# Moving the weight loads to one queue behind the first transposes, and reordering loads and statistics, in a linear-attention plus GeGLU block

## The chip, the cores and the metric

The kernel runs on one core of one Trainium2 chip. The metric is the device time of one execution in microseconds (us). Engines are named as the profile names them: PE is TensorE, DVE is VectorE, ACT is ScalarE, POOL is GpSimd, SP is SyncE, which here only issues DMAs and DMA transposes.

## The reference, cut to what matters

S = 2048 tokens, D = 448 features, FF = 1792, 16 heads of 28 features. All inputs are bf16.

```python
def _A_ref(x, wqkv, wo):
    q, k, v = split_heads(x @ wqkv)
    phi = lambda t: jnp.where(t > 0, t + 1, jnp.exp(t)) + 1e-6
    pq, pk = phi(q), phi(k)
    kv = jnp.einsum("bhsd,bhse->bhde", pk, v)
    z = jnp.einsum("bhsd->bhd", pk)
    num = jnp.einsum("bhqd,bhde->bhqe", pq, kv)
    den = jnp.einsum("bhqd,bhd->bhq", pq, z)[..., None] + 1e-6
    return merge_heads(num / den) @ wo

def _B_ref(x, w_gate, w_up, w_down):
    return (gelu(x @ w_gate) * (x @ w_up)) @ w_down

h = x + _A_ref(_layernorm(x), A_wqkv, A_wo)
h2 = h + _B_ref(_layernorm(h), B_w_gate, B_w_up, B_w_down)
```

B_x is not used. Two facts order the work. The linear attention needs kv and z summed over all 2048 tokens before the first output, and every matmul that contracts over features needs the normalised tile transposed.

## The kernel before, in words

The 2048 tokens are 16 tiles of 128. The work falls into three stages that overlap.

**A1.** For each tile t: batch-norm statistics on DVE (`ln_stats`, L432 to L434), 1/sqrt on ACT (`ln_rstd_act`, L441), then the normalisation into a slot of `xn` (XN_R = 6 slots), on DVE for the first four tiles (L467) and on POOL after them (L470), and a copy of the last 64 columns on DVE (`dup`, L472). The transposition into `xnT` is done by PE and a DVE evacuation for the first four tiles (L480, L483, one PSUM bank, 7) and by a DMA transpose issued from SP for the other twelve (L485). Then follow the K and V projections (`fk`, L496, and `fv`, L504 to L508; tiles 0 and 1 alone, the rest in pairs), the feature map of K (exp on ACT L522, clip on POOL L525, `pk` on DVE L527), the evacuation of V on ACT (L529) and the sum of kv (`fnacc`, L535). K has four PSUM banks, V two. The 16 Q projections (L560, four tiles and a quarter of the features each) have their own exp, clip and `pqT` (L563 to L565).

**A2.** For each tile (`a2_tile`, L568): numerator and denominator (L580), the division (L583, L584), the transposition of the result (PE for tiles 0 and 1, L594; a DMA transpose from SP for the rest, L599), the product with wo (L607), the residual (L610), the second statistics, the second normalisation (L622 or L625), a copy that doubles the row (`wrap`, L627) and the transposition into `hnT` (PE with an ACT evacuation for tiles 0 and 1, L634 and L637; DMA transposes from SP for the rest, L640).

**B.** `gu_chunk` (L665): gate and up products in 64-row halves of PE (L690, L692), gelu on ACT (L714), the product on DVE (L716). `b2_tile` (L644): the down product (L653), the residual (L657) and the store from SP (L659).

The order of each engine's instructions is static. `_Graph.schedule` (L91) simulates a list schedule: each operation has an estimated duration, its dependencies and a key, and of the operations that are ready on an engine the one with the smallest key goes first. The engines then run their lists in order, with semaphore waits. Keys that matter here: statistics and normalisation of tile t have key t - LN_LEAD with LN_LEAD = 4 (L458), the K and V work of a pair has the pair's first tile as key (L489), Q projections 11.5 for the first four and 17 for the rest (L555), the A2 work of tiles 0 and 1 has -60 (L571).

The loads. x comes in five DMAs: tile 0 on SP and tile 1 on ACT, then wv on SP, then tiles 2-3, 4-7, 8-11 and 12-15 on SP (L384 to L391); wq and wo follow on SP (L393 to L397). The MLP weights come in twelve pieces of 336 or 448 KB (`big_piece`, L362), issued from ACT's queue: one after each exp of a K tile, from tile 1 on (L523, T_W = 1).

Of the kernel before, what the change touches and what calls it, by code (L numbers as in the profile page):

```python
# [35 lines left out]
class _Graph:  # L36
# [186 lines left out]
def bass_sequential_preLN__linear_attn_block__glu_gated_geglu__prompt_kernel(  # L223
# [10 lines left out]
    XN_R = 6  # L234
# [8 lines left out]
    N_DVE_NORM = cfg.get("n_dve_norm", 4)  # L243
# [5 lines left out]
    T_W = cfg.get("t_w", 1)  # L249
    LN_LEAD = cfg.get("ln_lead", 4.0)  # L250
# [4 lines left out]
    K_Q0 = cfg.get("k_q0", 11.5)  # L255
    K_B1 = cfg.get("k_b1", 100.0)
# [5 lines left out]
    with es:  # L262
# [83 lines left out]
        BK_K, BK_V, BK_ACC, BK_TP = (0, 1, 2, 3), (4, 5), 6, 7  # L346
# [11 lines left out]
        def dma(out_ap, in_ap, w, name, nbytes, q="sp", key=None, r=(), after=()):  # L358
            ik[0] += 0.01
            return G.add(q, lambda e: e.dma_start(out_ap, in_ap), r=r, w=w, name=name, kind="dma", key=ik[0] if key is None else key, nbytes=nbytes, after=after)  # L360

        def big_piece(n, key, after):  # L362
            p_ = n // 2 if n < 8 else n - 8
            a_, c_ = JS[p_]
            cs = slice(a_ * 128, c_ * 128)
            nb = (c_ - a_) * 128 * D * 2
            if n >= 8:
                dma(wd_sb[:, a_:c_, :], B_w_down[cs, :].rearrange("(j p) n -> p j n", p=128), [b_wd[p_]], "dwd%d" % p_, nb, q="act", key=key, after=[after])
            elif n % 2 == 0:
                dma(wgu_sb[0:64, :, cs], B_w_gate[:, cs].rearrange("(k p) n -> p k n", p=64), [b_wg[p_]], "dwg%d" % p_, nb, q="act", key=key, after=[after])  # L370
            else:
                dma(wgu_sb[64:128, :, cs], B_w_up[:, cs].rearrange("(k p) n -> p k n", p=64), [b_wu[p_]], "dwu%d" % p_, nb, q="act", key=key, after=[after])
# [82 lines left out]
        xn_bufs = lambda t: [b_xnT[t]]  # L455

        for ts in STAT_GROUPS:
            kln = float(ts[0]) - LN_LEAD  # L458
# [5 lines left out]
            for t in ts:  # L464
# [8 lines left out]
                tok = slice(t * 128, (t + 1) * 128)  # L473
                if t < N_PE_TR:
                    tv = psb[:, BK_TP, 0:512].rearrange("p (k t) -> p k t", k=4)
# [6 lines left out]
                    G.add("pe", ftr, r=[b_xn[sl], b_xnd[sl], b_ident], w=bank(BK_TP), name="tr%d" % t, dur=_c_mm(128, 4), lat=PE_L, key=t - 3.0)  # L482
                    op("dve", lambda e, tok=tok, tv=tv: e.tensor_copy(xnT[:, :, tok], tv), bank(BK_TP), xn_bufs(t), "ev%d" % t, 0.33, t - 3.0)  # L483
                else:
                    G.add("sp", lambda e, tok=tok, sl=sl: e.dma_start_transpose(xnT[:, :, tok], xn[:, sl, :]), r=[b_xn[sl], b_xnd[sl]], w=xn_bufs(t),  # L485
                          name="xT%d" % t, kind="dmat", dur=1.25, lat=1.3, key=t - 3.0)

        for pair in PAIRS:
# [27 lines left out]
            for t in pair:  # L516
# [6 lines left out]
                if 0 <= t - T_W < 12:  # L523
                    big_piece(t - T_W, kk, ek)
# [43 lines left out]
        def a2_tile(t):  # L568
# [58 lines left out]
            op("dve", lambda e, sh=sh: e.tensor_copy(hn[:, sh, D:2 * D], hn[:, sh, 0:D]), [b_hn[sh]], [b_hnd[sh]], "wrap%d" % t, 0.18, ka)  # L627
            if t < N_PE_A2:
                tvh = psb[:, bth, 0:896].rearrange("p (k t) -> p k t", k=7)

                def ftrh(e, sh=sh, tvh=tvh):
                    ins = None
                    for k in range(7):
                        ins = e.transpose(tvh[:, k, :], hn[:, sh, k * 128:(k + 1) * 128], ident[:])  # L634
                    return ins
                G.add("pe", ftrh, r=[b_hn[sh], b_hnd[sh], b_ident], w=bank(bth), name="trh%d" % t, dur=_c_mm(128, 7), lat=PE_L, key=ka)
                op("act", lambda e, t=t, tvh=tvh: e.activation(hnT[:, :, (t % HR) * 128:(t % HR + 1) * 128], tvh, AF.Identity), bank(bth), [b_hnT[t % HR]],  # L637
                   "evh%d" % t, _c_act(896), ka)
            else:
# [4 lines left out]
        def b2_tile(t, split):  # L644
# [10 lines left out]
            G.add("pe", fnd, r=[(b_ar[j][t % HR], j if j >= split else 0) for j in range(NJ)] + [(b_wd[j2p[j]], j) for j in range(NJ)], w=bank(bk), name="down%d" % t,  # L655
# [9 lines left out]
        def gu_chunk(t0, nt):  # L665
# [6 lines left out]
            while j0 < NJ:  # L672
# [22 lines left out]
                G.add("pe", fngu, r=[b_hnT[t % HR] for t in tiles] + [(b_wg[j2p[j0 + jj]], 14 * jj) for jj in range(nj)] + [(b_wu[j2p[j0 + jj]], 14 * jj + 1) for jj in range(nj)], w=[(b_ps[BK_G[i]], 0), (b_ps[BK_U[i]], 1)], name="gu%d" % v,  # L695
# [96 lines left out]
```

## Time and profile before

| what | us |
|---|---|
| median of 3 runs | 214.25 |
| lowest and highest of the runs | 212.67, 215.92 |
| the profiled execution, its own time | 214.05 |
| its span in the trace | 212.3 |
| PE busy | 198.1 (93%) |
| DVE busy | 123.2 (58%) |
| ACT busy | 70.8 (33%) |
| POOL busy | 54.5 (26%) |

The span is from the first to the last recorded instruction; 1.75 us of the profiled execution's time lie outside it. PE busy counts matmuls at whatever clock they ran at, so time lost to a low clock hides in it and must be read from the granted clock.

### The profile page before, as it was taken

Reading aid. Unit: us, or ns where it says so; the run is one execution under the profiler, and the core shown is the slowest. Engines: PE = TensorE matmul, PEld = TensorE weight load, DVE = VectorE, ACT = ScalarE, POOL = GpSimd, SP = SyncE. Lnnn points to the kernel's source line nnn. Section 1 sums busy time; section 2 is a strip of 40 time slices with the busy share of each in tenths; the row PEclk is TensorE's granted clock in tenths of the full one; section 3 lists DMA queues with packets and bytes.
Section 4 is the critical chain, followed back from the end, with each engine's and each line's share of the span. In section 5 each row is a group of like instructions: output and inputs, shape, how many; then the busy total and the mean of one; then the engine's idle time right before and its main releaser. Section 6 shows DMA issues by size and latency. Waiting matters only on the chain.

```text
span 212.3 us, 4508 instructions
## 1 busy us (share of the span) xinstructions
PE 198.1 (93%) x1666; PEld 113.1 (53%) x1666; DVE 123.2 (58%) x320; ACT 70.8 (33%) x190; POOL 54.5 (26%) x121
## 2 busy tenths in 40 slices
PE   8688399998977999999999999999999999999994
PEld 7342155455645777577654466554455554464452
DVE  4899514429996668778878745422545422454422
ACT  3345335474683232022310344300434300434200
POOL 4069535336343143443354410010000000000000
PEclk9999979999997999999999999999999999999999
DMA  6987999920102244485554000461000001000011
GB/s 199 348 202 162 179 211 191 299 72 0 22 6 49 46 91 74 90 120 108 75 106 76 22 2 3 76 139 44 6 0 3 0 29 47 14 0 5 0 43 43
DMA packets 40470, 17.00 MB, mean 80 GB/s; under 512 B 29633, under 2 KB 40449, under 8 KB 40449
## 3 DMA queue, kind: packets, MB, share of 16 engines
q1 hardware_dynamic: 34256, 11.39, 27.5%
q10 hardware_dynamic: 6192, 5.33, 10.5%
q8 instruction: 13, 0.21, 0.4%
q14 instruction: 9, 0.07, 0.1%
HBM read 8.26 MB, written 1.84 MB: 48 GB/s over the span
## 4 chain that ended last, share of the span: by engine, by line
PE 83%; DVE 9%; DMA 5%; ACT 1%; issue 1%; POOL 0%; DVEq 0%; POOLq 0%; ACTq 0%
PE ps L690 34%; PE ps L653 20%; PE ps L692 8%; PE ps L607 6%; PE ps L560 5%; DVE st L433 3%; DMA xnT<-xn 3%; PE ps L504 3%; PE ps L496 3%; PE ps L580 2%; PE ps L535 2%; DMA x_sb<-in_A_x_dram 1%; PE ps L507 1%; DVE pqT L565 1%; DVE pk L527 1%
## 5 line engine op out<-in xcount | busy, mean ns | idle before, releaser
L692 PE MATMUL ps<-hnT,wgu_sb 64*128 64x512 bf16 (+1 forms) x490 | 89.0, 339 | 0.0
L690 PE MATMUL ps<-hnT,wgu_sb 64*128 64x512 bf16 (+1 forms) x490 | 88.7, 338 | 0.0
L714 ACT ACTIVATE gl<-ps 128x256 bf16<-128x256 f32 x112 | 37.1, 381 | 97.8 <-PE ps L692 48.4
L716 DVE TENSOR_TENSOR hh<-ps,gl 128x256 bf16<-128x256 f32 x112 | 42.4, 420 | 39.5 <-ACT gl L714 39.1
L690 PEld LDWEIGHTS ps<-hnT,wgu_sb 64*128 64x128 bf16 x490 | 45.7, 96 | 24.8 <-issue 1.5
L692 PEld LDWEIGHTS ps<-hnT,wgu_sb 64*128 64x128 bf16 x490 | 43.7, 96 | 8.4 <-DVE hh L716 3.2
L653 PE MATMUL ps<-wd_sb,hh 128*128 128x448 bf16 x224 | 43.6, 353 | 0.0
L653 PEld LDWEIGHTS ps<-wd_sb,hh 128*128 128x128 bf16 x224 | 21.5, 98 | 20.5 <-issue 1.3
L657 DVE TENSOR_TENSOR x_sb<-ps,x_sb 128x448 bf16<-128x448 f32 x16 | 10.0, 624 | 23.4 <-PE ps L653 23.4
L433 DVE BATCH_NORM_STATS2 st<-x_sb 128x6 f32<-128x448 bf16 x32 | 19.0, 605 | 1.3 <-DMA x_sb<-in_A_x_dram 1.2
L560 PE MATMUL ps<-xnT,wq_sb 128*113 128x512 bf16 x64 | 16.7, 395 | 0.0
L527 DVE SCALAR_TENSOR_TENSOR pk<-ps,tm 128x448 bf16<-128x448 f32 x16 | 9.4, 619 | 10.7 <-POOL tm L525 10.7
L496 PE MATMUL ps<-wkv_sb,xnT 128*128 128x448 bf16 x48 | 11.4, 365 | 4.4 <-DMA xnT<-xn 2.8
L607 PE MATMUL ps<-wo_sb,oT 128*128 128x448 bf16 x64 | 14.6, 354 | 0.0
L625 POOL TENSOR_SCALAR hn<-x_sb,nm,rs 128x448 bf16<-128x448 bf16 x14 | 10.0, 716 | 16.9 <-DMA hnT<-hn 15.5
L525 POOL TENSOR_SCALAR tm<-e 128x448 bf16<-128x448 bf16 x16 | 8.8, 562 | 19.0 <-ACT e L522 18.3
L563 ACT ACTIVATE e<-ps 113x512 bf16<-113x512 f32 x16 | 9.5, 600 | 12.2 <-PE ps L560 12.2
L438 POOL TENSOR_SCALAR nm<-mv 128x1 f32<-128x1 f32 (+1 forms) x20 | 4.7, 235 | 33.6 <-DVE mv L434 33.6
L564 POOL TENSOR_SCALAR tm<-e 113x512 bf16<-113x512 bf16 x16 | 9.8, 614 | 7.7 <-ACT e L563 6.0
L565 DVE SCALAR_TENSOR_TENSOR pqT<-ps,tm 113x512 bf16<-113x512 f32 x16 | 10.6, 678 | 1.4 <-POOL tm L564 1.4
L504 PE MATMUL ps<-wkv_sb,xnT 128*128 128x448 bf16 x48 | 10.7, 357 | 0.0
L529 ACT ACTIVATE v<-ps 128x448 bf16<-128x448 f32 x16 | 7.9, 541 | 7.5 <-PE ps L508 7.3
(60 smaller groups left out, 153.8 us busy)
## 6 DMA issues: line engine op xcount, KB each, us to landing
out_dram<-x_sb SPq DMA_DIRECT2D x16, 112.0 KB, 1.7
x_sb<-in_A_x_dram SPq DMA_DIRECT2D x3, 448.0 KB, 5.6
wgu_sb<-in_B_w_gate_dram ACTq DMA_DIRECT2D x2, 448.0 KB, 6.6
wgu_sb<-in_B_w_up_dram ACTq DMA_DIRECT2D x2, 448.0 KB, 5.2
wd_sb<-in_B_w_down_dram ACTq DMA_DIRECT2D x2, 448.0 KB, 5.8
wgu_sb<-in_B_w_gate_dram ACTq DMA_DIRECT2D x2, 336.0 KB, 6.3
wgu_sb<-in_B_w_up_dram ACTq DMA_DIRECT2D x2, 336.0 KB, 6.2
wd_sb<-in_B_w_down_dram ACTq DMA_DIRECT2D x2, 336.0 KB, 4.0
```

What stands on the lines that cost most here:

```text
L433: op("dve", lambda e: e.bn_stats(st[:, t, :], src_ap), [b_src], [b_st[t]], "bnst%d" % t, 0.53, key)
L496: ins = e.matmul(ps[:, BK_K[t % 4], 0:D], xnT[:, k, t * 128:(t + 1) * 128], wkv_sb[:, k, 0:D], start=(k == 0), stop=False)
L504: ins = e.matmul(ps[:, BK_V[t % 2], 0:D], xnT[:, k, t * 128:(t + 1) * 128], wkv_sb[:, k, D:2 * D], start=(k == 0), stop=False)
L527: op("dve", lambda e, i=i, ie=ie, psK3=psK3: e.scalar_tensor_tensor(pk[:, i, :, 1:GP], psK3, EPS, tm1[:, ie, :].rearrange("p (g e) -> p g ...
L560: ins = e.matmul(psQ, wq_sb[:, k, g, 1:GP + 1], xnT[:, k, c * QCH:(c + 1) * QCH], start=(k == 0), stop=(k == 3))
L565: op("dve", lambda e, i=i, c=c, g=g, psQ=psQ: e.scalar_tensor_tensor(pqT[:, g, c * QCH:(c + 1) * QCH], psQ, EPS, tm2[:, i, :], ALU.max, AL ...
L607: ins = e.matmul(psH, oT[:, so, g, :], wo_sb[:, g, :], start=(g == 0), stop=(g == 3))
L653: ins = e.matmul(psO, hh[:, j, (t % HR) * 128:(t % HR + 1) * 128], wd_sb[:, j, :], start=(j == 0), stop=(j == NJ - 1))
L690: e.matmul(psG[:, jj * N:(jj + 1) * N], wgu_sb[A_, k, j * 128:(j + 1) * 128], hnT[A_, ka_, c0:c0 + N], start=(k == 0), stop=(k == 6))
L692: ins = e.matmul(psU[:, jj * N:(jj + 1) * N], wgu_sb[B_, k, j * 128:(j + 1) * 128], hnT[B_, kb_, c0:c0 + N], start=(k == 0), stop=(k == 6))
L714: G.add("act", lambda e, gi=gi, cs_=cs_, psG=psG: e.activation(gl[:, gi, cs_], psG[:, cs_], AF.Gelu_apprx_tanh), r=bank(BK_G[i]), w=[b_glh ...
L716: op("dve", lambda e, dst=dst, srcU=srcU, srcL=srcL: e.tensor_tensor(dst, srcU, srcL, ALU.mult), bank(BK_U[i]) + [b_glh], [b_ar[j_][t % HR ...
```

## The change

The loads of the MLP weights and of wo leave their places: the twelve pieces on ACT's queue become three whole loads (gate, up, down), and they and wo are issued from SP, in the order gate, up, wo, down, after the last DMA transpose of `xn`, which are now kept in tile order. x tiles 2-3 are loaded ahead of wv, and tiles 4-7 in two loads. `xn` has one slot for each tile. LN_LEAD goes from 4 to 8, so that the statistics of tile t come ahead of the K work of tile t - 8 in the list, and those of tiles 0 and 1 ahead of everything (30 lower). Tiles 2 and 3 are normalised on POOL, and their PE transposes are evacuated by ACT; the PE transposes alternate between banks 7 and 3. The memset of `wq_sb` goes from DVE to POOL. In A2's first two tiles the `wrap` copies 64 columns and not 448, PE reads the shifted blocks directly, and the `hnT` evacuation of tile 1 goes to DVE. In the scheduler, an order-only dependency no longer delays the ready time, and the load of x tile 1 is given 0.5 us more.

```diff
-    XN_R = 6
+    XN_R = 16
-    N_DVE_NORM = cfg.get("n_dve_norm", 4)
+    N_DVE_NORM = cfg.get("n_dve_norm", 2)
+    N_DVE_EV = cfg.get("n_dve_ev", 2)
-    T_W = cfg.get("t_w", 1)
-    LN_LEAD = cfg.get("ln_lead", 4.0)
+    LN_LEAD = cfg.get("ln_lead", 8.0)
-        BK_K, BK_V, BK_ACC, BK_TP = (0, 1, 2, 3), (4, 5), 6, 7
+        BK_K, BK_V, BK_ACC, BK_TP = (0, 1, 2, 3), (4, 5), 6, (7, 3)
...
             for s_ in t.succ:
-                s_.ready = max(s_.ready, t.finish + SEM_LAT[s_.eng])
+                if t in s_.deps:
+                    s_.ready = max(s_.ready, t.finish + SEM_LAT[s_.eng])
...
+        dma_x(0, 1)
+        dma_x(1, 2, q="act", lat=0.5)
+        dma_x(2, 4)
         dma(wkv_sb[:, 0:3, 0:D], ..., "dwk", 384 * D * 2, q="act")
         dma(wkv_sb[:, 0:3, D:2 * D], ..., "dwv", 384 * D * 2)
-        for a, b in ((2, 4), (4, 8), (8, 12), (12, 16)):
-            dma(x_sb[:, a:b, :], xv[:, a:b, :], b_x[a:b], "dx%d" % a, (b - a) * 128 * D * 2)
-        op("dve", lambda e: e.memset(wq_flat, 0.0), [], b_wq, "wq0", 0.97, key=-200.0)
+        dma_x(4, 6)
+        dma_x(6, 8)
+        dma_x(8, 12)
+        dma_x(12, 16)
+        op("pool", lambda e: e.memset(wq_flat, 0.0), [], b_wq, "wq0", 1.9, key=-250.0)
...
-            kln = float(ts[0]) - LN_LEAD
+            kln = float(ts[0]) - LN_LEAD - (30.0 if ts[0] < 2 else 0.0)
...
+                    if t < N_DVE_EV:
                         op("dve", ... e.tensor_copy(xnT[:, :, tok], tv), bank(btp), xn_bufs(t), "ev%d" % t, 0.33, ktr)
+                    else:
+                        op("act", ... e.activation(xnT[:, :, tok], tv, AF.Identity), bank(btp), xn_bufs(t), "ev%d" % t, _c_act(512), ktr)
...
+        wl = dict(after=xts[-1:], key=20.0)
+        dma(wgu_sb[0:64, :, :], B_w_gate.rearrange("(k p) n -> p k n", p=64), [b_wg], "dwg", D * FF * 2, **wl)
+        dma(wgu_sb[64:128, :, :], B_w_up.rearrange("(k p) n -> p k n", p=64), [b_wu], "dwu", D * FF * 2, **wl)
+        dma(wo_sb[:, 0:3, :], ..., [b_wo[0]], "dwo", 384 * D * 2, **wl)
+        dma(wo_sb[0:64, 3, :], A_wo[384:448, :], [b_wo[1]], "dwo_t", 64 * D * 2, **wl)
+        dma(wd_sb[:, :, :], B_w_down.rearrange("(j p) n -> p j n", p=128), [b_wd], "dwd", FF * D * 2, **wl)
...
-                if 0 <= t - T_W < 12:
-                    big_piece(t - T_W, kk, ek)
...
             if t < N_PE_A2:
+                op("dve", ... e.tensor_copy(hn[:, sh, D:512], hn[:, sh, 0:64]), ..., "wrap%d" % t, 0.09, ka)
...
+                if t % 2 == 0:
                   op("act", ... "evh%d" % t, _c_act(896), ka)
+                else:
+                  op("dve", ... "evh%d" % t, 0.55, ka)
```

## Rows read from the trace of the kernel before

**Rows 1.** Busy time by stage: us, busy of each engine (count), granted clock, DMA share, GB/s.

```profile
7.68:25.50 17.82, 12.46 (x79) 5.41 (x77) 16.03 (x51) 9.34 (x29) 11.25 (x22) 1.00 1.01 199
25.50:30.40 4.90, 4.90 (x21) 2.32 (x21) 0.76 (x4) 0.60 (x1) 2.90 (x5) 0.65 1.20 214
30.40:45.60 15.20, 15.20 (x109) 7.85 (x107) 6.43 (x11) 8.49 (x18) 5.56 (x10) 1.00 0.98 221
45.60:50.00 4.40, 3.76 (x29) 2.42 (x30) 2.25 (x5) 3.06 (x7) 2.24 (x4) 1.00 0.00 0
50.00:61.90 11.90, 11.88 (x79) 7.32 (x77) 11.46 (x27) 7.37 (x17) 5.53 (x10) 1.00 0.06 12
61.90:65.48 3.58, 0.88 (x12) 0.62 (x13) 3.21 (x8) 2.87 (x3) 1.32 (x4) 1.00 0.00 0
65.48:70.10 4.62, 4.62 (x56) 3.54 (x56) 1.92 (x5) 0.66 (x2) 1.01 (x2) 0.63 0.54 104
70.10:209.60 139.50, 139.46 (x1250) 78.99 (x1244) 76.32 (x199) 36.40 (x110) 22.56 (x52) 1.00 0.24 46
```

**Rows 2.** The chain that ended last, 0 to 70 us: start, length, what.

```profile
17.83 0.43 DVE st L433
18.25 7.11 DMA xnT<-xn
```

**Rows 3.** DMA issues: tile, queue, count, KB each, median us from issue to landing.

```profile
wkv_sb<-in_A_wqkv_dram SPq DMA_DIRECT2D x1, 336.0 KB, 4.1
...
oT<-o_sb SPq DMA_TRANSPOSE x14, 2.4
...
xnT<-xn SPq DMA_TRANSPOSE x12, 6.4
```

**Rows 4.** Who waited for whom: total us, times, longest us.

```profile
POOL tm L525 <- ACT e L522: 18.3, 6, 7.4
...
POOL xn L470 <- DMA xnT<-xn: 2.3, 2, 1.3
```

**Rows 5.** One tile's or line's instructions: ns minimum/median/maximum, first and last start.

```profile
L433 DVE BATCH_NORM_STATS2 st<-x_sb x16: 586/610/627, 3.6 to 19.5; 128x6 f32<-128x448 bf16 x16
L467 DVE TENSOR_SCALAR xn<-x_sb,mv,rs x4: 380/385/395, 5.6 to 10.9; 128x448 bf16<-128x448 bf16 x4
L470 POOL TENSOR_SCALAR xn<-x_sb,nm,rs x12: 715/717/723, 12.8 to 28.4; 128x448 bf16<-128x448 bf16 x12
L472 DVE COPY xn<-xn x16: 150/178/552, 6.2 to 29.2; 128x64 bf16<-128x64 bf16 x16
L485 SPq DMA_TRANSPOSE xnT<-xn x12: 1204/1226/3396, 14.3 to 31.5; - x12
```

**Rows 6.** Groups by line, 0 to 50 us: count, busy us, mean ns, idle before.

```profile
L527 DVE SCALAR_TENSOR_TENSOR pk<-ps,tm 128x448 bf16<-128x448 f32 x16 | 9.4, 619 | 10.7 <-POOL tm L525 10.7
L407 POOL MEMSET o_sb<- 128x192 bf16 x1 | 0.3, 258 | 0.0
```

**Rows 7.** Timeline of the start: start us, length, instruction.

```profile
1.25 1.02 SPq L360 DMA_DIRECT2D wkv_sb<-in_A_wqkv_dram  x2
8.24 0.73 PE L504 MATMUL ps<-wkv_sb,xnT 128*128 128x448 bf16 x3
```

**Rows 8.** Busy time in two stretches in which weight pieces were loading, as rows 1.

```profile
22.00:24.00 2.00, 0.73 (x3) 0.22 (x3) 0.63 (x3) 1.44 (x5) 1.35 (x3) 1.00 1.38 152
...
40.00:42.00 2.00, 2.00 (x13) 0.83 (x11) 1.25 (x2) 0.60 (x1) 1.42 (x3) 1.00 1.08 361
```

**Rows 9.** Timeline ahead of the first gate and up products.

```profile
56.62 11.09 SPq L599 DMA_TRANSPOSE oT<-o_sb  x3
59.33 0.92 PE L607 MATMUL ps<-wo_sb,oT 128*128 128x448 bf16 x4
62.11 0.52 DVE L627 COPY hn<-hn 128x448 bf16<-128x448 bf16 x1
63.06 1.73 ACT L637 ACTIVATE hnT<-ps 128x896 bf16<-128x896 bf16 x2
```

More of the change, by code (lines that the diff above doesn't have):

```diff
@@ L323, in bass_sequential_preLN__linear_attn_block__glu_gated_geglu__prompt_kernel @@
         b_wo = bufs("wo", 3)
-        JS = [(0, 4), (4, 7), (7, 11), (11, 14)]
-        j2p = [p_ for p_, (a_, c_) in enumerate(JS) for _ in range(a_, c_)]
-        b_wg, b_wu, b_wd = bufs("wg", 4), bufs("wu", 4), bufs("wd", 4)
+        b_wg, b_wu, b_wd = _Buf("wg"), _Buf("wu"), _Buf("wd")
         b_ident, b_ones, b_mask2, b_mask3, b_mtmp, b_mones = (_Buf(n) for n in ("ident", "ones", "mask2", "mask3", "mtmp", "mones"))
@@ L356, in bass_sequential_preLN__linear_attn_block__glu_gated_geglu__prompt_kernel, with dma @@
         ik = [-300.0]
-        def dma(out_ap, in_ap, w, name, nbytes, q="sp", key=None, r=(), after=()):
+        def dma(out_ap, in_ap, w, name, nbytes, q="sp", key=None, r=(), after=(), lat=0.0):
             ik[0] += 0.01
[L360 to L372, printed above, removed]
+            return G.add(q, lambda e: e.dma_start(out_ap, in_ap), r=r, w=w, name=name, kind="dma", key=ik[0] if key is None else key, nbytes=nbytes, after=after, lat=lat)
         def op(eng, fn, r, w, name, dur, key=None, lat=None):
@@ L427, in warm_fn @@
             for _ in range(WARM):
-                ins = e.matmul(ps[:, BK_TP, 0:128], ones_bf[:], ones_bf[:], start=True, stop=True)
+                ins = e.matmul(ps[:, BK_TP[1], 0:128], ones_bf[:], ones_bf[:], start=True, stop=True)
             return ins
-        G.add("pe", warm_fn, r=[b_ones], w=bank(BK_TP), name="warm", dur=WARM * 0.1, key=-100.0)
+        G.add("pe", warm_fn, r=[b_ones], w=bank(BK_TP[1]), name="warm", dur=WARM * 0.1, key=-100.0)
         def ln_stats(t, src_ap, b_src, st, mv, b_st, b_mv, key):
@@ L481, in ftr @@
                         return ins
[L482 to L486 removed]
+                    G.add("pe", ftr, r=[b_xn[sl], b_xnd[sl], b_ident], w=bank(btp), name="tr%d" % t, dur=_c_mm(128, 4), lat=PE_L, key=ktr)
+                    if t < N_DVE_EV:
+                        op("dve", lambda e, tok=tok, tv=tv: e.tensor_copy(xnT[:, :, tok], tv), bank(btp), xn_bufs(t), "ev%d" % t, 0.33, ktr)
+                    else:
+                        op("act", lambda e, tok=tok, tv=tv: e.activation(xnT[:, :, tok], tv, AF.Identity), bank(btp), xn_bufs(t), "ev%d" % t, _c_act(512), ktr)
+                else:
+                    xt = G.add("sp", lambda e, tok=tok, sl=sl: e.dma_start_transpose(xnT[:, :, tok], xn[:, sl, :]), r=[b_xn[sl], b_xnd[sl]], w=xn_bufs(t),
+                          name="xT%d" % t, kind="dmat", dur=1.25, lat=1.3, key=t - 3.0, after=xts[-1:])
+                    xts.append(xt)
+        wl = dict(after=xts[-1:], key=20.0)
+        dma(wgu_sb[0:64, :, :], B_w_gate.rearrange("(k p) n -> p k n", p=64), [b_wg], "dwg", D * FF * 2, **wl)
+        dma(wgu_sb[64:128, :, :], B_w_up.rearrange("(k p) n -> p k n", p=64), [b_wu], "dwu", D * FF * 2, **wl)
+        dma(wo_sb[:, 0:3, :], A_wo[0:384, :].rearrange("(g p) n -> p g n", p=128), [b_wo[0]], "dwo", 384 * D * 2, **wl)
+        dma(wo_sb[0:64, 3, :], A_wo[384:448, :], [b_wo[1]], "dwo_t", 64 * D * 2, **wl)
+        dma(wd_sb[:, :, :], B_w_down.rearrange("(j p) n -> p j n", p=128), [b_wd], "dwd", FF * D * 2, **wl)
         for pair in PAIRS:
@@ L626, in a2_tile @@
                [b_h[t], b_nm2[t], b_rs2[t]], [b_hn[sh], b_hnd[sh]], "normh%d" % t, 0.70, ka)
[L627 removed]
             if t < N_PE_A2:
+                op("dve", lambda e, sh=sh: e.tensor_copy(hn[:, sh, D:512], hn[:, sh, 0:64]), [b_hn[sh]], [b_hnd[sh]], "wrap%d" % t, 0.09, ka)
                 tvh = psb[:, bth, 0:896].rearrange("p (k t) -> p k t", k=7)
@@ L632, in ftrh @@
                     ins = None
-                    for k in range(7):
-                        ins = e.transpose(tvh[:, k, :], hn[:, sh, k * 128:(k + 1) * 128], ident[:])
+                    for k in (0, 1, 2, 4, 5, 6, 3):
+                        ko = k * 128 if k < 4 else (k - 4) * 128 + 64
+                        ins = e.transpose(tvh[:, k, :], hn[:, sh, ko:ko + 128], ident[:])
                     return ins
                 G.add("pe", ftrh, r=[b_hn[sh], b_hnd[sh], b_ident], w=bank(bth), name="trh%d" % t, dur=_c_mm(128, 7), lat=PE_L, key=ka)
-                op("act", lambda e, t=t, tvh=tvh: e.activation(hnT[:, :, (t % HR) * 128:(t % HR + 1) * 128], tvh, AF.Identity), bank(bth), [b_hnT[t % HR]],
-                   "evh%d" % t, _c_act(896), ka)
+                if t % 2 == 0:
+                    op("act", lambda e, t=t, tvh=tvh: e.activation(hnT[:, :, (t % HR) * 128:(t % HR + 1) * 128], tvh, AF.Identity), bank(bth), [b_hnT[t % HR]],
+                       "evh%d" % t, _c_act(896), ka)
+                else:
+                    op("dve", lambda e, t=t, tvh=tvh: e.tensor_copy(hnT[:, :, (t % HR) * 128:(t % HR + 1) * 128], tvh), bank(bth), [b_hnT[t % HR]],
+                       "evh%d" % t, 0.55, ka)
             else:
+              op("dve", lambda e, sh=sh: e.tensor_copy(hn[:, sh, D:2 * D], hn[:, sh, 0:D]), [b_hn[sh]], [b_hnd[sh]], "wrap%d" % t, 0.18, ka)
               G.add("sp", lambda e, t=t, sh=sh: e.dma_start_transpose(hnT[:, :, (t % HR) * 128:(t % HR + 1) * 128], hn[:, sh, :]), r=[b_hn[sh], b_hnd[sh]], w=[b_hnT[t % HR]],
@@ L654, in fnd @@
                 return ins
-            G.add("pe", fnd, r=[(b_ar[j][t % HR], j if j >= split else 0) for j in range(NJ)] + [(b_wd[j2p[j]], j) for j in range(NJ)], w=bank(bk), name="down%d" % t,
+            G.add("pe", fnd, r=[(b_ar[j][t % HR], j if j >= split else 0) for j in range(NJ)] + [b_wd], w=bank(bk), name="down%d" % t,
                   dur=_c_mm(D, NJ), lat=PE_L, key=kd, mw=True)
@@ L694, in fngu @@
                     return ins
-                G.add("pe", fngu, r=[b_hnT[t % HR] for t in tiles] + [(b_wg[j2p[j0 + jj]], 14 * jj) for jj in range(nj)] + [(b_wu[j2p[j0 + jj]], 14 * jj + 1) for jj in range(nj)], w=[(b_ps[BK_G[i]], 0), (b_ps[BK_U[i]], 1)], name="gu%d" % v,
+                G.add("pe", fngu, r=[b_hnT[t % HR] for t in tiles] + [b_wg, (b_wu, 1)], w=[(b_ps[BK_G[i]], 0), (b_ps[BK_U[i]], 1)], name="gu%d" % v,
                       dur=_c_mm(N, 7 * nj), lat=PE_L, key=kb, mode=64, mw=True)
```

18 lines of the change are left out of this document (10 added, 8 removed).

## The prediction

> **What bounds the kernel now.** I read the page's 40 slices first: PE is near full nearly everywhere except in a few slices before 70 us. So the second view is busy time by stage, cut where those slices change [rows 1]. From 70.10 to 209.60 us PE is busy 139.46 of 139.50 us at full clock: no edit here gives it less to do, so what the change can win lies before 70 us. There the lost time is:
>
> - 7.68 to 25.50: 17.82 - 12.46 = 5.36 us idle, while DVE is busy 16.03 of 17.82;
> - 25.50 to 30.40: PE always busy, but at a granted clock of 0.65, between its two levels 1.2 and 2.4 GHz; at full clock this work takes 4.90 x 0.65, so 1.7 us are lost. What PE did before was wait;
> - 45.60 to 50.00: 0.64 us idle;
> - 61.90 to 65.48: 3.58 - 0.88 = 2.70 us idle, DVE busy 3.21 of 3.58;
> - 65.48 to 70.10: clock 0.63, so 4.62 x 0.37 = 1.7 us lost, again just behind a wait.
>
> Together 12.1 us. (The stretch before 7.68 us is the first load and two tiles' latency and stays.) Third view, the chain of waits [rows 2]: up to 18.25 us it is DVE's statistics, then one piece of 7.11 us that is a DMA transpose of xn, then PE to the end of A1. Fourth, the DMA issues [rows 3]: the same kind of transpose takes 6.4 us to land in A1 and 2.4 us in A2, where no weight piece is loading. Fifth, the waits [rows 4]: POOL waited 2.3 us for a transpose to give a slot of xn back. So the first loss has two causes in series: DVE is full until about 22 us, and behind it the transposes are slow and few.
>
> **Weights off the path of the transposes.** In the time of the twelve transposes (issued from 14.3 us to beyond 31.5, one taking 3.4 us to issue where 1.2 is the rule [rows 5]) about half of the twelve pieces are loading on the other queue. Afterwards none is. A transpose then lands 2.4 us after issue instead of 6.4, the row of A2 being the nearest one. The floor is SP's issue: 12 x 1.23 = 14.8 us. The first can go at about 11.5 us: 14.3 less 1.6 us of relief on DVE (below) less two `pk` of 0.62 us [rows 6] that now stand behind tile 4's statistics. The last is then issued by about 26 to 27 us and landed by 29, one tile each 1.23 us. PE needs more than that: in the full stretch from 30.40 to 45.60 us it did the work of eight tiles and two Q projections in 15.20 us [rows 1], 1.9 us a tile. So the transposes no longer hold it. With 16 slots POOL's 2.3 us wait goes too.
>
> The Trainium skill, in "DMA: Bandwidth & Descriptors", section "Queues, rings and completion order", says that each DMA engine goes round between the queues that have work, packet by packet, and takes one ring's descriptors in order. The trace agrees with the first half (6.4 against 2.4 us). The second half speaks against the change: what SP issues later, the transposes of A2, stands behind all of the weights. That is the rival on the slow side, worked out below from rows.
>
> **Statistics first, and DVE's relief.** Two normalisations (0.385 us each [rows 5]) and two evacuations of about the same length leave DVE: 1.6 us. The wq memset leaves it in a time in which it waits for x, worth nothing. LN_LEAD adds no work but moves it: four more tiles' statistics (0.61), small aggregations and `dup` copies (0.18 to 0.55) now go ahead of a `pk`, some 3.8 us, so the first `pk` come about 2 to 3 us later than now, and kv sums with them. PE has two pairs of K and V (four K banks) and one Q projection to do meanwhile, about what those us hold; then the third pair needs bank 0, that is the first `pk`. From there DVE must hand over one `pk` per 1.9 us and has its relief. DVE was busy 16.03 of 17.82 us; less 1.6 and with about four `pk` more that the faster PE asks for in this stretch (4 x 0.62 = 2.5) it is busy 16.9: it fits, with no room. So not all 5.36 us go. Bounds: 0.5 us left (every wait covered) and 4 us left (the transposes gone as a cause, DVE the sole limit: about the 5.36 less the piece of wait on transposes that follows 24 us). I take 1.5, nearer the low end, because the longest wait is the one whose cause goes. Gain 3.9. With no long wait ahead of it the clock should stay up in what is now 25.50 to 30.40: gain 1.7 (0 if the idle remains).
>
> POOL takes two normalisations of 0.72 us and the memset. It is idle for 7.4 us before its first clip [rows 4], and its memset of 192 elements took 0.258 us [rows 6], so 928 or 1856 elements cost 0.9 to 2.5 us, between 1 and 4 us of the timeline: hidden. In 7.68 to 25.50 it is busy 11.25 of 17.82; with 1.4 and more clips it stays under full. ACT gets two evacuations of about the same 0.5 us and loses twelve DMA issues; at 9.34 of 17.82 it isn't the limit. A gain below nothing is possible where `dup` meets POOL's normalisation: its copies take 0.18 us alone and 0.55 beside POOL [rows 5], for two more tiles 0.7 us at most, within the 4 us bound.
>
> The Trainium skill, "SBUF — State Buffer", states that DVE's two-port copies and POOL exclude each other for a whole instruction. The spread 0.18 to 0.55 agrees. By this rule all of the moved normalisations would come back as DVE waits, 2 x 0.37 = 0.7 us, the bound just named.
>
> **x before wv.** One load of 224 KB now goes ahead of wv: some 0.5 us of issue and 224 KB at the 250 GB/s of a loading stretch, 0.9 us. wv was issued at 1.25 us [rows 7] and landed 4.1 us later [rows 3], at 5.4; then at 6.8, and the first V matmul starts at 8.24 [rows 7]. Covered by 1.4 us; if not, PE starts V later by the excess.
>
> **The weights' new time.** Gate, up and down are 1.61 MB each and wo 0.40: 5.22 MB from about 27 us on. The bounds for the rate are the two stretches with pieces loading [rows 8]: 152 GB/s beside transposes, 361 with hardly any. Afterwards there are none beside them, so I am nearer the upper row and take 300: all landed after 17.4 us, at 44 us (41.5 at 361, 61 at 152). gate, up and wo (3.61 MB) land at 39 (37 to 51). wo is needed some 5 us before the first A2 transpose, which SP issues at 56.62 us now [rows 9], or at about 50 after the gain; gate and up at 59. So covered at my rate and wo 4 to 6 us late at the lowest.
>
> **Between A2's start and the first gate product.** The two `wrap` copies shrink from 448 to 64 columns; the second took 0.52 [rows 9] and a 64-column copy 0.18, so 0.3 us each of which one lies on the path. The two `hnT` evacuations, 1.73 us in series on ACT [rows 9], run side by side: 0.87 less, against one DVE step of 0.55 that DVE, busy 3.21 of 3.58 us, has to fit. Together 0.9 us of the 2.70 (0 to 2). That leaves 1.8 us idle, and I count the low clock behind it (1.7 us) as staying.
>
> **Sum.** 3.9 + 1.7 + 0.9 = 6.5 us. From the profiled execution's 214.05 us (its span of 212.3 and 1.75 around it; 0.2 under the runs' median) that is 207.5. Own range 204 to 211: all of the first idle, the clock behind 65 us and the second idle won as well would be near 11 us; with 4 us idle left in A1 the gain is 1.4 + 0.8 + 0.9 = 3.1, 211.
>
> **The rivals.**
>
> *The gain is eaten at A1's end.* If K and V run faster, fewer Q projections are used as filler before 45 us and more come behind, and from 50.00 to 65.48 us DVE is busy 14.67 of 15.48 [rows 1]. Four more `pqT` of some 0.65 us there would give back 2.6 us: gain 3.9, about 210. For it: DVE's share there. Against: PE's 2.70 us idle there is itself room for these projections. Or statistics first leaves 4 us idle in A1 (above): 211. Chance 0.22 for the two.
>
> *The transposes stay slow.* Twelve in a row on one ring, behind the wq loads, may queue upon each other and not upon the weights. Then only the slots and DVE's relief count, 2 us: 212. For it: one of them takes 3.4 us to issue. Against: those of A2 land in 2.4 us. Chance 0.06.
>
> *Slower: A2's transposes behind the weights.* The weights load at the lower row's 152 GB/s, end at 61.3 us, and the first oT transpose lands 2.4 us later, at 63.7. The product with wo that waits for it stands in PE's list at 59.33 us [rows 9], ahead of the first gate product; it starts 4.4 us later than now: 218.5. It decides as soon as the down weights land behind 57 us (5.22 MB in 30 us, 175 GB/s); between 175 and 226 GB/s it only eats the gain. For it: no row shows one queue moving these long rows into 64 partitions alone. Against: the 361 GB/s. Chance 0.12.
>
> **How the numbers follow.** Forecast 0.60, the rivals 0.22, 0.06 and 0.12. About 2% (4.3 us) is what a measurement of this kernel can tell from no change; faster by that is under 209.8. The forecast gives nearly all of its 0.60 to it, A1's-end 0.10: faster 0.69. Within 2%: the rest of these and the slow transposes, 0.20. Slower: 0.11, nearly all of the last rival. The range of 203.5 to 213 leaves out the last rival and a little at the low end.
>
> **What would show it right or wrong.** Right: landing of xnT about 2.5 us; PE idle under 2.5 us in the stretch up to the eighth K tile, which starts near 24 us; no low clock near 25 to 30 us; first gate products at 58 to 60 us; the down weights landed before 50 us; the stage behind it still 139.5 us long. Wrong: landings near 6 us; PE waiting on `pk` for several us before 20 us with the clock falling there; wo or oT late with a weight load as the releaser; or a gate stage that starts early and ends no earlier.

## The result, and the profile after

The changed kernel takes 205.57 us (median of 4 runs, 204.97 to 207.52) where the kernel before, run beside it, takes 213.53 (212.67 to 215.92). The ratio is 0.966, with a 95% interval from 0.956 to 0.975. The profiled execution took 204.97 us, its span is 203.2 us.

Busy time by stage of the kernel after, cut at its own first K matmul (7.31 us), at the stretch that answers to the first two of [rows 1], and around its first gate product (57.53 us). The columns are those of [rows 1]: length, PE, PEld, DVE, ACT, POOL, granted clock, DMA share, GB/s.

```profile
7.31:25.05 17.74, 17.11 (x111) 8.35 (x112) 15.39 (x47) 11.65 (x33) 15.75 (x30) 1.00 0.71 140
...
38.40:42.80 4.40, 3.76 (x29) 2.42 (x30) 2.25 (x5) 3.06 (x7) 2.23 (x4) 1.00 1.03 203
42.80:54.60 11.80, 11.48 (x72) 6.77 (x71) 11.33 (x27) 6.66 (x15) 5.51 (x9) 1.00 0.82 214
54.60:57.53 2.93, 1.13 (x19) 0.82 (x16) 2.93 (x8) 2.80 (x3) 0.61 (x1) 1.00 0.00 0
57.53:62.00 4.47, 4.47 (x77) 4.04 (x78) 2.46 (x8) 1.32 (x4) 1.74 (x4) 1.00 0.20 34
62.00:200.20 138.20, 138.20 (x1232) 76.00 (x1226) 76.51 (x199) 35.74 (x108) 22.51 (x52) 1.00 0.26 49
```

Set against [rows 1], the span is 9.1 us shorter, and the parts add up to that. (Stage by stage the agreement is looser. From the first K matmul to the wait for the last `pk`, which starts the stretch from 45.60 us before and 38.40 after, 6.8 us are gained where the rows give 6.4; behind the first gate product it is 1.2 where they give 1.7.)

| part | before | after | gain |
|---|---|---|---|
| first K matmul starts | 7.68 | 7.31 | 0.4 |
| PE idle in the first K tiles | 5.36 | 17.74 - 17.11 = 0.63 | 4.7 |
| low clock behind it | 1.7 | 0 | 1.7 |
| wait for the last `pk` | 0.64 | 0.64 | 0 |
| PE idle ahead of the first gate product | 0.02 + 2.70 | 0.32 + 1.80 | 0.6 |
| low clock behind it | 1.7 | 0 | 1.7 |

The last row is no sure gain of the change: experiments 1, 2 and 6 to 10 show that the clock in this place stays up in some executions and falls in others.

The DMA side, from the tile views of `xnT`, `wgu_sb`, `wo_sb` and `wd_sb` of the kernel after (ns minimum/median/maximum, first and last start) and the page's DMA issues (KB, us to landing):

```profile
L483 SPq DMA_TRANSPOSE xnT<-xn x12: 1202/1217/2232, 11.1 to 26.6; - x12
...
DMA to landing us min/median/max: 2.4/2.5/4.8
...
L360 SPq DMA_DIRECT2D wo_sb<-in_A_wo_dram x2: 624/642/660, 29.2 to 29.9; - x2
...
L360 SPq DMA_DIRECT2D wd_sb<-in_B_w_down_dram x1: 588/588/588, 30.6 to 30.6; - x1
```

```profile
wgu_sb<-in_B_w_gate_dram SPq DMA_DIRECT2D x1, 1568.0 KB, 10.5
wgu_sb<-in_B_w_up_dram SPq DMA_DIRECT2D x1, 1568.0 KB, 18.6
wd_sb<-in_B_w_down_dram SPq DMA_DIRECT2D x1, 1568.0 KB, 21.6
```

The transposes of xn start at 11.1 us and not 14.3, land after 2.5 us and not 6.4 [rows 3], and the last is issued at 26.6. The weights end at 30.6 + 21.6 = 52.2 us: later than the 44 that the prediction took. PE wants wo at 48.25 us and the first oT at 52.8, so the weights came just in time.

### The profile page after: what moved, and what is told of

It reads as the page before. It is cut to its first block, busy times and chain, and to the rows that moved or that the text cites. A ratio compares the mean times of both kernels' runs of the same rounds, so it can differ in the third digit from the quotient of the medians.

```text
span 203.2 us, 4501 instructions
## 1 busy us (share of the span) xinstructions
PE 194.5 (96%) x1666; PEld 109.5 (54%) x1666; DVE 122.0 (60%) x316; ACT 71.1 (35%) x191; POOL 57.7 (28%) x126
## 3 DMA queue, kind: packets, MB, share of 16 engines
HBM read 8.26 MB, written 1.84 MB: 50 GB/s over the span
## 4 chain that ended last, share of the span: by engine, by line
PE 85%; DVE 9%; ACT 2%; issue 1%; DMA 1%; POOL 0%; POOLq 0%; DVEq 0%; ACTq 0%
PE ps L699 36%; PE ps L662 21%; PE ps L701 7%; PE ps L610 6%; PE ps L563 4%; PE ps L501 3%; DVE st L425 3%; PE ps L509 3%; PE ps L538 2%; PE ps L583 2%; DVE pk L530 1%; DMA x_sb<-in_A_x_dram 1%; PE ps L512 1%; DVE pqT L568 1%; DVE xn L465 1%
## 5 line engine op out<-in xcount | busy, mean ns | idle before, releaser
L699 PE MATMUL ps<-hnT,wgu_sb 64*128 64x512 bf16 (+1 forms) x490 | 87.1, 333 | 1.7 <-DVE mv L426 1.7
L701 PE MATMUL ps<-hnT,wgu_sb 64*128 64x512 bf16 (+1 forms) x490 | 87.4, 334 | 0.0
L699 PEld LDWEIGHTS ps<-hnT,wgu_sb 64*128 64x128 bf16 x490 | 44.8, 94 | 28.8 <-DVE mv L426 1.9
L701 PEld LDWEIGHTS ps<-hnT,wgu_sb 64*128 64x128 bf16 x490 | 42.8, 94 | 7.1 <-DVE hh L725 2.0
L563 PE MATMUL ps<-xnT,wq_sb 128*113 128x512 bf16 x64 | 15.8, 380 | 0.0
L628 POOL TENSOR_SCALAR hn<-x_sb,nm,rs 128x448 bf16<-128x448 bf16 x14 | 10.0, 714 | 15.1 <-DMA hnT<-hn 13.7
L501 PE MATMUL ps<-wkv_sb,xnT 128*128 128x448 bf16 x48 | 10.5, 352 | 0.5 <-DVE mv L426 0.5
L509 PE MATMUL ps<-wkv_sb,xnT 128*128 128x448 bf16 x48 | 10.5, 352 | 0.0
## 6 DMA issues: line engine op xcount, KB each, us to landing
wgu_sb<-in_B_w_gate_dram SPq DMA_DIRECT2D x1, 1568.0 KB, 10.5
wgu_sb<-in_B_w_up_dram SPq DMA_DIRECT2D x1, 1568.0 KB, 18.6
wd_sb<-in_B_w_down_dram SPq DMA_DIRECT2D x1, 1568.0 KB, 21.6
```

The source lines that it names most:

```text
L501: ins = e.matmul(ps[:, BK_K[t % 4], 0:D], xnT[:, k, t * 128:(t + 1) * 128], wkv_sb[:, k, 0:D], start=(k == 0), stop=False)
L509: ins = e.matmul(ps[:, BK_V[t % 2], 0:D], xnT[:, k, t * 128:(t + 1) * 128], wkv_sb[:, k, D:2 * D], start=(k == 0), stop=False)
L563: ins = e.matmul(psQ, wq_sb[:, k, g, 1:GP + 1], xnT[:, k, c * QCH:(c + 1) * QCH], start=(k == 0), stop=(k == 3))
L699: e.matmul(psG[:, jj * N:(jj + 1) * N], wgu_sb[A_, k, j * 128:(j + 1) * 128], hnT[A_, ka_, c0:c0 + N], start=(k == 0), stop=(k == 6))
L701: ins = e.matmul(psU[:, jj * N:(jj + 1) * N], wgu_sb[B_, k, j * 128:(j + 1) * 128], hnT[B_, kb_, c0:c0 + N], start=(k == 0), stop=(k == 6))
```

## The experiments

Each edit is made in the kernel after unless it says otherwise. "Order kept" means that every engine's list stays as it was, save for the DMAs named.

**1. Only the weights moved.** In the kernel before:

```diff
-                    big_piece(t - T_W, kk, ek)
-        dma(wo_sb[:, 0:3, :], ...)
+        dma(...)  # gate, up, wo, down on SP, after=[the last xT]
```

> The kernel before with one edit: the weight loads and wo go to SP behind the last transpose of xn (six slots, LN_LEAD 4, old loads of x, old A2). If the weights' traffic held the transposes: landing near 2.5 us, most of the first idle and of the first low clock gone, 208 to 210 us. If DVE's order was the limit: 212 to 214 us.

Measured: 209.5 us beside 214.6, ratio 0.976 (0.970 to 0.981). From its views by tile (`xnT`) and by stage:

```profile
L483 SPq DMA_TRANSPOSE xnT<-xn x12: 1202/1219/2042, 15.3 to 30.7; - x12
...
DMA to landing us min/median/max: 2.4/2.5/4.6
```

```profile
7.70:26.00 18.30, 15.36 (x92) 7.06 (x91) 16.49 (x52) 9.36 (x30) 12.33 (x24) 1.00 0.58 114
26.00:32.00 6.00, 6.00 (x45) 3.02 (x44) 3.10 (x6) 3.51 (x8) 2.92 (x5) 1.00 0.45 91
...
58.40:62.33 3.93, 1.49 (x24) 1.05 (x22) 3.46 (x9) 3.59 (x4) 1.41 (x4) 1.00 0.00 0
62.33:66.90 4.57, 4.57 (x73) 3.56 (x74) 2.85 (x8) 1.32 (x4) 0.95 (x2) 1.00 0.54 106
```

The landing is as short as in the kernel after, and the first low clock is gone; but the first transpose goes at 15.3 us, and 2.9 us of the 5.4 of idle stay, where most of it was expected to go. So the weights' traffic is a cause on its own, worth 4.1 us in this stretch (2.4 of idle, 1.7 of clock). The whole time fell by 5.1 us, and that holds something that was not expected: the last two rows are the ones around the first gate product (62.27 us), and behind 2.44 us of idle, with the old A2, the second low clock stayed away as well. That is another 1.7 us; other stages gave part of it back (the profiled executions differ by 4.9 us).

**2. All but the weights.** The twelve pieces on ACT and wo behind wq, as before; the rest is the change.

```diff
-        dma(wgu_sb[0:64, :, :], ..., after=xts[-1:], key=20.0)
+                if 0 <= t - 1 < 12:
+                    big_piece(t - 1, kk, ek)
```

> The changed kernel with the loads of the kernel before: twelve pieces on ACT's queue, one after each exp of K from tile 1 on, wo on SP behind wq; the planner orders anew. If the weights' traffic is the cause: landing of xnT 5 us or more, 208 to 212 us. If order, slots and DVE's relief are enough: 205 to 207 us.

Measured: 209.33 us beside 214.55, ratio 0.977 (0.972 to 0.981).

```profile
L499 SPq DMA_TRANSPOSE xnT<-xn x12: 1212/1236/3469, 11.1 to 28.7; - x12
...
DMA to landing us min/median/max: 3.5/6.7/9.9
```

```profile
7.30:23.00 15.70, 12.30 (x79) 5.75 (x79) 13.38 (x44) 9.92 (x29) 14.14 (x27) 1.00 1.18 235
23.00:27.00 4.00, 3.77 (x14) 1.29 (x14) 1.30 (x3) 0.00 (x0) 0.64 (x2) 0.59 1.15 233
...
58.00:61.63 3.63, 1.79 (x22) 1.14 (x19) 3.63 (x9) 2.80 (x3) 1.14 (x2) 1.00 0.00 0
61.63:66.20 4.57, 4.57 (x80) 4.16 (x82) 3.24 (x11) 1.32 (x4) 1.74 (x4) 1.00 0.20 41
```

The transposes are issued as early as after the whole change and land as late as before it. PE idles 3.6 us in the first two stretches, and 4.00 x 0.41 = 1.6 us go to the low clock: 5.2 us, against 7.1 before, 2.9 in experiment 1 and 0.6 after. So in this part of the kernel the two halves save 1.9 and 4.1 us, and both together 6.4: they add up, as two causes in series do. The whole times (5.2 and 5.1 us saved, together 8.0) seem to say otherwise. Most of that is again the second low clock: it stayed away in this profiled execution too, behind 1.84 us of idle, so both halves hold the same 1.7 us, which can be won only once.

**3. Whole loads early on ACT's queue**, order kept.

```diff
+        place("dwg", "act", "ek0")
+        place("dwu", "act", "ek1")
+        place("dwo", "act", "ek3")
+        place("dwd", "act", "ek5")
```

> The changed kernel with every engine's order kept; only the five weight loads are issued from ACT's queue, between the exps of the first K tiles (from about 11 us on), so that they load beside the transposes of xn. If the weights' traffic is what held the transposes: landing of xnT rises from 2.5 to 5 us or more, PE idles 3 to 6 us before 25 us, the clock falls behind it, 209 to 212 us. If the new order and the slots made the gain: within 1 us of the changed kernel, 205 to 207 us.

Measured: 224.76 us (221.34 to 225.18), ratio 1.038 (1.026 to 1.051). The sign was right, the size far off. Waits of PE, the tile view of `xnT` and a row of the DMA issues:

```profile
PE ps L501 <- DMA xnT<-xn: 14.1, 2, 12.9
```

```profile
L483 SPq DMA_TRANSPOSE xnT<-xn x12: 1190/1258/7681, 12.3 to 40.8; - x12
...
DMA to landing us min/median/max: 2.4/6.0/18.6
```

```profile
wgu_sb<-in_B_w_up_dram ACTq DMA_DIRECT2D x1, 1568.0 KB, 17.4
```

The first three transposes, issued from 12.3 to 15.1 us, took 17.6, 18.6 and 17.4 us and landed between 29.9 and 32.5 us. ACT had issued gate, up and wo (3.6 MB) from 11.7 to 17.0 us, and these landed at the same time: up at 13.0 + 17.4 = 30.4 us, wo near 32. (Down followed only at 36.9 us, behind its exp.) PE waited 12.9 us at a stretch. With the pieces of experiment 2 the worst landing was 9.9.

**4. Whole loads on SP ahead of the first transpose**, order kept; one execution.

```diff
+        place("dwg", "sp", "xT4", True)  # then dwu, dwo, dwo_t, dwd
```

> The changed kernel with every other order kept; the five weight loads stand on SP ahead of the first transpose of xn, on the same queue. If a queue's data go in order: the first transpose issued lands only behind 5.22 MB, at 215 GB/s near 34 us, where it landed at about 14; PE waits for it about 20 us, 222 to 228 us. If transposes slip past: as with the loads on ACT's queue, some of them early, PE busy in between.

Measured: 225.14 us.

```profile
PE ps L501 <- DMA xnT<-xn: 18.0, 1, 18.0
```

```profile
L483 SPq DMA_TRANSPOSE xnT<-xn x12: 1199/1218/18242, 12.9 to 45.2; - x12
...
DMA to landing us min/median/max: 2.4/2.6/22.2
...
wd_sb<-in_B_w_down_dram SPq DMA_DIRECT2D x1, 1568.0 KB, 22.5
```

One wait of 18.0 us, and SP itself stood 18.2 us in the issue of one transpose. That transpose landed at 12.9 + 22.2 = 35.1 us, the last weights (down, issued at 12.2) at 34.7: behind the weights on the same queue it waited for all of them, as expected. This is the slow rival's mechanism, at a place where it hurts.

**5. wo last.** Order kept; the loads go down, gate, up, wo.

> The changed kernel with the weights in the order down, gate, up, wo; every other order stays. All 5.22 MB still land at about 52 us, so wo lands 4 us behind the time at which PE first wants it (48.25 us): PE waits 3.5 to 4.5 us there and the clock may fall behind it, 209 to 211 us. If wo's time is not what PE starts from: no change.

Measured: 213.4 us, ratio 0.996 (0.991 to 1.000): slower than expected.

```profile
PE ps L610 <- DMA wo_sb<-in_A_wo_dram: 4.0, 1, 4.0
```

```profile
48.50:52.60 4.10, 0.07 (x2) 0.06 (x2) 1.24 (x3) 0.75 (x2) 0.61 (x1) 0.80 0.81 150
52.60:57.70 5.10, 5.10 (x14) 2.38 (x15) 2.57 (x6) 0.16 (x1) 0.00 (x0) 0.50 0.00 0
...
61.00:64.14 3.14, 1.30 (x20) 0.84 (x16) 3.14 (x8) 2.80 (x3) 0.69 (x2) 1.00 0.00 0
64.14:68.10 3.96, 3.96 (x42) 3.58 (x44) 1.98 (x6) 0.66 (x2) 1.74 (x4) 0.57 0.19 37
```

The wait is the 4.0 us that was worked out. Behind it PE runs at half its clock for 5.1 us (2.6 us lost), and the clock falls again behind the 1.84 us of idle ahead of the first gate product (3.96 x 0.43 = 1.7 us lost). The three make up the 8.3 us by which the two profiled executions differ (213.28 and 204.97). The order of these five loads alone is worth 7.8 us in the medians, nearly all of the change's gain; 1.7 of it is the second low clock, which other orders lose in some executions too (experiments 6 to 10).

**6 to 9. One part undone each.**

```diff
-    XN_R = 16
+    XN_R = 6
```

> The changed kernel with six slots of xn and not sixteen; every engine's order stays. With the transposes landing in 2.5 us a slot is free long before it is needed: within 0.3 us of the changed kernel. If the slots were a cause of their own: POOL waits on transposes again, 1 to 2 us longer.

```diff
-    LN_LEAD = cfg.get("ln_lead", 8.0)
+    LN_LEAD = cfg.get("ln_lead", 4.0)
```

> The changed kernel with LN_LEAD 4 and not 8. If statistics first matters: tiles 4 on are normalised later, the first DMA transpose goes later than 11.1 us, PE idles 1 to 2 us more, 206.5 to 208 us. If the two orders only trade one wait for another: within 0.5 us.

```diff
-    N_DVE_NORM = cfg.get("n_dve_norm", 2)
-    N_DVE_EV = cfg.get("n_dve_ev", 2)
+    N_DVE_NORM = cfg.get("n_dve_norm", 4)
+    N_DVE_EV = cfg.get("n_dve_ev", 4)
...
-        op("pool", lambda e: e.memset(wq_flat, 0.0), ...)
+        op("dve", lambda e: e.memset(wq_flat, 0.0), ...)
```

> The changed kernel with four normalisations and four evacuations on DVE again, and the wq memset too. If DVE is the limit before 20 us: the 1.6 us of work come back as 1 to 2 us. If the slack is enough: within 0.5 us.

```diff
-  ... e.tensor_copy(hn[:, sh, D:512], hn[:, sh, 0:64]) ...      # hnT evacuation of tile 1 on DVE
+  ... e.tensor_copy(hn[:, sh, D:2 * D], hn[:, sh, 0:D]) ...      # both on ACT
```

> The changed kernel with the old first two tiles of A2: 448 columns in the wrap and both evacuations of hnT on ACT. If these edits removed the second fall of the clock: PE idle ahead of the first gate product is 2.5 us or more again, the clock falls behind it, 2 to 3 us longer (207.5 to 208.5). If the fall went for another reason: 0.5 to 1 us longer, clock up.

| undone | median us | runs | ratio to before, interval |
|---|---|---|---|
| 16 slots | 205.83 | 205.5 to 207.48 | 0.960 (0.953 to 0.966) |
| LN_LEAD 8 | 207.01 | 205.83 to 210.16 | 0.964 (0.958 to 0.970) |
| DVE's relief | 206.29 | 205.18 to 207.70 | 0.963 (0.956 to 0.970) |
| A2's edits | 207.11 | 205.76 to 207.62 | 0.964 (0.958 to 0.971) |

None is told apart from the change's 0.966 by its interval. Six slots cost nothing that these runs show, as expected, once the transposes land quickly. With LN_LEAD 4 the first DMA transpose goes at 13.3 us and not 11.1; that is seen in the trace, but the 1 to 2 us expected for it are not shown: the executions at full clock took 205.83 and 206.28 us, against 204.97 to 205.59 of the kernel after. With DVE's relief undone they took 205.18 and 205.39, so the relief shows no gain either. With the old A2, PE's idle ahead of the first gate product is 2.53 us again, as expected; the clock fell behind it in the profiled execution, and in two of the four it stayed up. The loads of x, the second PSUM bank of the PE transposes and the scheduler's rule were not undone by themselves.

The single executions say more than the medians. In these kernels most of them fall into two sorts: those with a mean granted clock of 0.998 and above, and those near 0.99 or below, mostly 1.5 to 2.5 us longer (relief undone: 205.18 and 205.39 at 1.0, 207.20 and 207.70 at 0.990 and 0.983). Two don't fit: 206.14 at 0.992 with six slots, 210.16 at 0.984 with LN_LEAD 4. The kernel after has one run of the second sort among four, its 207.52 at 0.982. The profiled execution with six slots, whose engines' lists are those of the kernel after, shows one place where the difference lies:

```profile
55.00:58.22 3.22, 1.41 (x19) 0.94 (x17) 3.22 (x8) 2.80 (x3) 0.81 (x2) 1.00 0.00 0
58.22:63.00 4.78, 4.75 (x56) 4.40 (x56) 2.36 (x7) 0.66 (x2) 1.75 (x4) 0.64 0.14 27
```

The same 1.81 us of idle ahead of the first gate product as the kernel after's 1.80, and behind it a clock of 0.64, which costs 1.7 us; in the kernel after it was 1.00. With the relief undone and in experiment 10 the clock fell here too, to 0.63 behind 1.79 us of idle each; in experiments 1 and 2 it stayed up behind 2.44 and 1.84 us. The profiled execution with LN_LEAD 4 kept its clock here and lost it in another place, at the start, after PE had been busy for 0.62 of the 2 us from 5 to 7:

```profile
7.00:11.00 4.00, 3.67 (x13) 1.61 (x13) 3.95 (x15) 1.28 (x4) 1.83 (x4) 0.57 1.17 329
```

The kernel after was busy for 0.81 of these 2 us, and its clock stayed at 1.00. What decides between the two outcomes is not shown.

**10. Gate and up on two queues.** Order kept.

```diff
+        place("dwu", "act", "ek11")
```

> The changed kernel; only the load of up goes from ACT's queue, at about 28 us, while gate goes from SP. Gate and up fill different halves of the 128 partitions. If a load into 64 partitions is held to some 210 GB/s by its half, both together run at 350 and all weights land at about 43 to 45 us and not 52; PE's small waits for wo and the first oT go, 0 to 0.7 us less. If the rate is held by something else, they land near 52 and the time stays.

Measured: 206.04 us, ratio 0.962 (0.956 to 0.968), and the weights end at 30.0 + 22.3 = 52.3 us. ACT issued up at 31.4 us, with gate still loading. A stretch in which both were loading, first of this kernel, then of the kernel after, with the one in which wo and down follow the last of up:

```profile
34.00:38.00 4.00, 4.00 (x29) 1.97 (x27) 1.68 (x4) 2.25 (x5) 1.63 (x3) 1.00 1.02 200
```

```profile
34.00:38.00 4.00, 4.00 (x30) 1.90 (x29) 1.67 (x4) 1.93 (x5) 1.70 (x3) 1.00 1.05 214
...
46.00:50.00 4.00, 3.94 (x30) 2.27 (x28) 3.96 (x9) 2.64 (x5) 1.84 (x3) 1.00 1.09 357
```

200 against 214 GB/s: that each is held by its half of the partitions alone falls, since then up could have loaded beside gate at its own rate. It hardly did: gate landed 11.0 us after its issue, against 10.5 without up on the other queue. What holds the rate stays open.

**11 and 12. A version that should beat the kernel after.** In its trace the ACT evacuation of `hnT` stands behind the load of the gelu table:

```profile
55.22 1.28 ACT L742 ACT_TABLE_LOAD   x1
...
56.51 0.92 ACT L642 ACTIVATE hnT<-ps 128x896 bf16<-128x896 bf16 x1
```

```diff
-  after=exp_tasks)          # of the table load
+  after=exp_tasks + evhs)   # evhs: that evacuation
```

> The changed kernel with the ACT evacuation of hnT for tile 0 ahead of the load of the gelu table. In the trace the evacuation is ready near 55.2 us, waits 1.28 us for the table and ends at 57.43, when the first gate product starts. Ahead of it, DVE's evacuation (to 56.81) sets the start: 0.6 to 0.8 us less, and the clock falls less often behind the shorter wait: 204 to 205 us. If the wait is DVE's: no change.

> Both edits, the evacuation ahead of the table load and the load of up on ACT's queue: the sum of the two, 0.6 to 1.5 us less than the changed kernel, 204 to 205 us.

Measured: 204.97 us (204.29 to 206.09, six runs), ratio 0.956 (0.951 to 0.962); with the two queues 204.88 (204.75 to 208.36), ratio 0.957 (0.952 to 0.963). In the first one's trace the evacuation runs at 56.14 us and the table load behind it, at 57.08, and PE's last wait there is 1.1 us for DVE where it was 1.7; all idle ahead of the gate product is 1.43 us where it was 1.80. The medians lie 0.6 us under the kernel after's, the size expected; the intervals overlap, so it is likely and not settled. Whether the clock falls less often behind the shorter wait is not shown: it stayed up there in the first one's profiled execution (and fell at 7 to 11 us), and fell there, behind 1.83 us, in the second one's.

## Why the prediction was right, and where its terms were off

The forecast of 207.5 us stood on a gain of 6.5 us; the profiled executions differ by 9.1, the medians by 8.0. In its own terms: 3.9 + 1.7 + 0.9 + 0 was said, 4.7 + 1.7 + 0.6 + 1.7 came, and 0.4 us at the start that it had not counted. Step by step:

- *The transposes land in 2.4 us once the weights are off their path.* Right: 2.5. Experiments 1 and 2 show that the traffic sets this, whatever the order (2.5 and 6.7 us). The first goes at 11.1 us (11.5 said), the last at 26.6 (26 to 27).
- *Of the first idle 1.5 us stay.* 0.63 stayed; the term gave 4.7 us and not 3.9. The prediction had the first `pk` 2 to 3 us later. It came 0.6 us later, 12.28 us against 11.70, and the second 1.3 us later (14.47 against 13.16); why so little was not taken apart. Experiments 1 and 2 bear out that two causes lie in series: either half alone leaves 2.9 and 3.6 us of idle, and what they save adds up.
- *The clock stays up behind it.* Right, 1.7 us.
- *0.9 us ahead of the first gate product.* 0.6. The two evacuations ran side by side, and the one on ACT then stood behind the table load, which the prediction left out; experiment 11 wins 0.4 us of idle by moving it.
- *The low clock behind 65 us stays.* This is the step that was mis-sized: 0 was counted, the profiled execution gained 1.7 us. The runs show that this is no property of the kernel alone: with like waits the clock falls in some executions and not in others, and in experiment 1 it stayed up even with the old A2. So the prediction had the cost right (1.7 us) and counted it as staying where it comes and goes between executions: the six-slot execution in which the clock did fall took 207.48 us, the forecast's number. It is most of what lies between 207.5 and 205.57.
- *The gain is eaten at A1's end.* Fell: DVE was as busy there as before (11.33 of 11.80 us, 11.46 of 11.90 before), and PE's idle there still went down, from 2.72 to 2.12 us.
- *All weights landed at 44 us, at 300 GB/s.* Wrong by 8 us: 5.22 MB from 27.9 to 52.2 us are 215 GB/s. That lies in the band of 175 to 226 GB/s in which the prediction had it eat part of the gain. It cost nearly nothing (PE waited 0.3 us for the first oT), but the slow rival was closer than its chance said: its point of decision was 57 us, and experiment 5 shows that 4 us at wo would have taken nearly the whole gain.

Of its signs two came out otherwise: the down weights landed at 52.2 us and not before 50, and the first gate product at 57.5, half a microsecond ahead of the stated 58 to 60.

## What to carry to other kernels

Loads that nobody needs yet should not run beside small DMA transposes that the matmul engine waits for: put them behind the last transpose, and order them by first use, since on one queue a late first use costs all the bytes ahead of it. Price an idle gap of the matmul engine together with the stretch at half clock that may follow it; here a wait of 4.0 us cost 6.6 with the low clock right behind it. Price the halves of a change in the stretches on which they act, and not by whole times alone: here the savings in the first stretch added up (1.9 and 4.1 of 6.4 us), and the whole times (5.2 and 5.1 of 8.0) seemed not to, mostly since both held the same clock gain, one that comes and goes between executions. And where a low clock comes and goes between executions of one kernel, compare executions at the same clock.

## What was not expected of the hardware

- Gate and up (rows of 3584 bytes into 64 partitions) loaded at 200 to 228 GB/s in stretches of 4 us. The stretch from 46 to 50 us, with wo and down (rows of 896 bytes into 128) behind the last of up, had 357. With down first (experiment 5) the rates turned round with the loads, 309 and then 206:

```profile
32.00:36.00 4.00, 4.00 (x29) 2.10 (x28) 1.85 (x3) 2.27 (x6) 1.69 (x3) 1.00 1.09 309
36.00:40.00 4.00, 4.00 (x32) 2.22 (x31) 1.16 (x2) 2.54 (x6) 1.08 (x2) 1.00 1.03 206
```

  A second queue didn't help. Row length and partitions weren't varied apart, so the cause stays open.
- 3.6 MB queued as whole loads on ACT's queue within 6 us held SP's first three transposes 17.4 to 18.6 us, until about the time at which those loads had landed, much as on the same queue (22.2); twelve pieces of 336 and 448 KB held them 9.9 at most. The Trainium skill, "DMA: Bandwidth & Descriptors", section "Queues, rings and completion order", has the engines go round between queues packet by packet. From that I had expected a fair share for the transposes; with whole loads experiment 3 shows none for the first three. Whether the length of the rows or the depth of the queue makes the difference wasn't tried.
- After like waits of 1.8 us the granted clock fell to half in some executions (0.64 and 0.63 in the stretch behind) and stayed at 1.00 in others. Such a fall costs 1.7 us here, about the scatter of most of these kernels' runs.
